# The gate of a top-1 MoE on column groups of TensorE, and GpSimd's two-input work on VectorE

## The chip, the cores and the metric

One core of a Trainium2 chip runs the whole kernel. The metric is the device time of one execution in microseconds; lower is better. TensorE is called PE here, VectorE DVE, ScalarE ACT, GpSimd POOL and SyncE, which issues most DMAs, SP, as in the profile.

## The reference

Three layers follow one another, for B = 4 batches, H = 8 heads, S = 768 positions, D = 48, so 3072 tokens of 384 numbers:

```python
state = f[:, :, t, :, None] * state + einsum('bhd,bhe->bhde', k[:, :, t], v[:, :, t])  # f = sigmoid(f_logit)
y[:, :, t] = einsum('bhd,bhde->bhe', q[:, :, t], state)
...
h = x @ w_in                        # 384 -> 2048
x = (h * sigmoid(h)) @ w_out        # 2048 -> 384
...
logits = x @ w_gate                 # 384 -> 8 experts
expert_idx = argmax(logits, axis=1)
gate_w = softmax(logits)[arange(N), expert_idx]
for e in range(8):                  # each token goes to one expert only
    out[mask] = gate_w[mask, None] * (np.maximum(x[mask] @ w1[e], 0.0) @ w2[e])   # 384 -> 1024 -> 384
```

All inputs and outputs are fp32.

## The kernel before

The tokens are cut into 24 chunks of 128 (n = 0 to 23), and the chunks into nine groups g of 2, 2, 3, 3, 3, 3, 3, 3 and 2 chunks, which are called tiles t of their group. The middle layer of a group takes 16 slots, one for each 128 columns of `w_in`. In a slot (`moe_h`, `moe_g`, `moe_o`) PE computes nine `ph` records, ACT and DVE turn them into the activated values `sg` and split these into a high part `gh` (a cast on ACT, L513) and a low part `gl` (a subtraction on DVE, L514), and PE multiplies them into `px` two slots later. Every weight and value is split that way (`w_hi`, `w_lo`; `xth`, `xtl`), and three products stand for one.

The attention layer, the loads and the routing are functions that a table (`at`, `at_end`, from L1093) puts into slots. PE's instructions keep the order in which the program issues them; for DVE, ACT, POOL and SP a scheduler chooses an order beforehand, and each then works in order. `ph` has two PSUM banks, `px` three, and all else three.

When a group's `px` is complete, `moe_x2` copies its tiles to SBUF. Then, one tile a slot, `flip_rows` turns a tile with three PE transposes into a PSUM bank `plt` and ACT copies it to `rt` (L579); `gate`, at the end of the same slot, multiplies the turned tile by the gate's weights `wgc` (L582 to L586):

```python
for c in range(KC):
    pe.matmul(pt[:, DM : DM + E], rt[:, c, :], wgc[:, c, :], start=c == 0, stop=c == KC - 1)
nc.vector.tensor_copy(lgt[g][:, t, :], pt[:, DM : DM + E])
```

The first operand of a matmul behind the output is the stationary one, the second the moving one. So `rt`, 128 by 128, is stationary, and 8 columns move; an fp32 matmul is two records in the trace. One slot behind the last tile `pick` finds each token's expert with small DVE operations (and an Exp on ACT), and RD = 4 slots later `route` counts the ranks on PE and scatters each token's row into `xs` in DRAM (a POOL DMA, L666). The last group, 8, takes other functions (`logits_pe`, `logits_pe2`).

`load_expert_unit` loads pieces of an expert's weights (`w_raw`, by SP), casts them on ACT (L228) and subtracts (L229). In slots 4, 6, 8 and 10 of group 8 it does so for expert 0, and `preload` behind the slots for half of expert 1; both give POOL the subtraction. `head_fetch`, in slot HF0 = 137 (slot 9 of group 8), reads the first rows of the first expert, `xe_h`, from `xs` (SP), and DVE casts their token numbers, `oi_h` (L775). `head_turn` turns these rows on PE (`pxs_h`).

POOL also multiplies the attention's state by the decay (L465, for n in `STP`, 1 to 7; 10 instructions) and makes `xtl` from n = 7 on (L477, 17 instructions).

Of the kernel before, what the change touches and what calls it, by code (L numbers as in the profile page):

```python
# [9 lines left out]
F32 = mybir.dt.float32  # L10
# [22 lines left out]
FC = 3  # L33
ORD = 1
AMP = ()
STP = (1, 2, 3, 4, 5, 6, 7)
PI = 12
PO = 12
LF = -27
# [47 lines left out]
FAR = float(1 << 20)  # L87
HEAD = 2
YT = 7
YLO = 1  # L90
CAPS = 512, 480, 432, 416, 400, 384, 376, 368
TINY = 2.0**-15

# [2 lines left out]
def kernel(  # L96
# [46 lines left out]
    def bank(kind, name):  # L143
        return ps.tile([P, 512], F32, tag=kind, name=name, bufs={"h": 2, "x": 3, "a": 3}[kind])
# [15 lines left out]
    state_all = state[:, : NPR * 112].rearrange("p (r e) -> p r e", r=NPR)  # L160
    qpads = [const.tile([P, H, 64], F32, name=f"qpad{i}") for i in range(2)]
    kpads = [const.tile([P, H, 64], F32, name=f"kpad{i}") for i in range(2)]
    wgc = const.tile([P, KC, E], F32, name="wgc")
    big = late.tile([P, 6 * 512], F32R, tag="big", name="big")
    xt0 = [big[:, i * 2 * DM : (i + 1) * 2 * DM].rearrange("p (r c t) -> p r c t", r=2, c=KC) for i in range(2)]
    zrow = big[:, 4 * DM : 4 * DM + ROW].bitcast(F32)
# [242 lines left out]
    def att4(n):  # L409
# [47 lines left out]
        for j in range(2):  # L457
            rows, cols = slice(64 * j, 64 * j + D), slice(0, D)
            ab = a_all[rows, n, :, None].to_broadcast([D, NPR, D])
            s = state_all[rows, :, 64 * j : 64 * j + D]  # L460
            if first:
                nc.vector.tensor_tensor(out=s, in0=pu3[rows, :, cols], in1=ab, op=ALU.mult)
            else:
                nc.vector.tensor_tensor(out=s, in0=pu3[rows, :, cols], in1=s, op=ALU.add)
                (nc.gpsimd if n in STP else nc.vector).tensor_tensor(out=s, in0=s, in1=ab, op=ALU.mult)  # L465

    def att5(n):
        g, r = group_of[n]
        if r == 0:
            xt[g] = xt0 if g == 0 else tuple(  # L470
                att.tile([P, CPG, KC, P], F32R, tag=f"xt{s}", name=f"xt{s}_{g}", bufs=2) for s in ("h", "l")
            )
        xh, xl = xt[g]
        y = ysb.pop(n)
        if n >= YT:
            nc.scalar.copy(xh[:, r], y)
            (nc.gpsimd if YLO else nc.vector).tensor_sub(xl[:, r], y, xh[:, r].bitcast(F32))  # L477
            return
        pt = use(n, 7, f"pt_{n}")
        for c in range(KC):  # L480
            pe.transpose(pt[:, c * P : (c + 1) * P], y[:, c, :], ident)
        pt3 = pt[:, :DM].rearrange("p (c t) -> p c t", c=KC)
        nc.scalar.copy(xh[:, r], pt3)
        nc.vector.tensor_sub(xl[:, r], pt3, xh[:, r].bitcast(F32))  # L484
# [76 lines left out]
    def logits_pe2(g):  # L561
        for t, rt in enumerate(rts):
            pl = bank(LB, f"plg_{g}_{t}")
            for c in range(KC):
                pe.matmul(pl[:, :E], rt[:, c, :], wgc[:, c, :], start=c == 0, stop=c == KC - 1)
            nc.vector.tensor_copy(lgt[g][:, t, :], pl[:, :E])

    flipped = {}
# [2 lines left out]
    def flip_rows(g, t):  # L571
        r = x2[starts[g] + t]
        pt = bank("a", f"plt_{g}_{t}")
        for c in range(KC):
            pe.transpose(pt[:, c * P : (c + 1) * P], r[:, c * P : (c + 1) * P], ident)
        if not turned_rows:
            turned_rows.append(late.tile([P, 4, KC, P], F32, tag="big", name="rt"))
        rt = turned_rows[0][:, (starts[g] + t) % 4]
        nc.scalar.copy(rt.rearrange("p c t -> p (c t)"), pt[:, :DM])  # L579
        flipped[g, t] = pt, rt  # L580

    def gate(g, t):  # L582
        pt, rt = flipped.pop((g, t))
        for c in range(KC):
            pe.matmul(pt[:, DM : DM + E], rt[:, c, :], wgc[:, c, :], start=c == 0, stop=c == KC - 1)
        nc.vector.tensor_copy(lgt[g][:, t, :], pt[:, DM : DM + E])  # L586

    picked = {}

# [336 lines left out]
    def general():  # L926
# [44 lines left out]
        with tc.tile_pool(name="g2", bufs=1) as gp, tc.tile_pool(name="g2p", bufs=1, space=PSUM) as pp:  # L971
# [17 lines left out]
            with tc.For_i(0, NT, P) as n0:  # L989
# [29 lines left out]
                x2T = flip(xr, "x2T")  # L1019
                pl = pp.tile([P, 512], F32, name="pl")  # L1020
                for c in range(KC):
                    nc.tensor.matmul(pl[:, :E], x2T[:, c, :], wgc[:, c, :], start=c == 0, stop=c == KC - 1)
                sh = gp.tile([P, E], F32, name="sh")
                oh = gp.tile([P, E], F32, name="oh")
                mx = gp.tile([P, 1], F32, name="mx")
# [41 lines left out]
    def consts():  # L1067
# [58 lines left out]
    for g in range(NG - 1):  # L1126
        s0 = {0: L0, 1: L1}.get(g, pos[g, NF - 1] + LAG + 1)
        for t in range(sizes[g]):
            at(s0 + t, flip_rows, g, t)
            at_end(s0 + t, gate, g, t)  # L1130
        s0 += sizes[g]
        at(s0, pick, g)
        at(s0 + RD, route, g)
        if g == NG - 3:
            at(s0 + RD + 1, rank_first)
            at(s0 + RD + 3, lambda: load_ids(ranks[0], (0, 1)))
# [5 lines left out]
    at(HF0, head_fetch)  # L1142
    at(NG * NF - 1, head_turn)
    for j in range(4):
        at(NG * NF - NF + 4 + 2 * j, load_expert_unit, (("w1", "w2")[j // 2], 0, j % 2), nc.gpsimd)
    at(6, lambda: nc.sync.dma_start(out=wgc, in_=moe2_w_gate.rearrange("(c p) e -> p c e", p=P)))

    def empty_row():
        tc.keep_in_program_order(nc.gpsimd.memset(zrow, 0.0))
# [52 lines left out]

    def preload():
        for j in range(2):
            load_expert_unit(("w1", 1, j), nc.gpsimd)

    todo = dict(
        o=lambda: moe_o(*outs.pop(0)), f=lambda: fill(1), F=lambda: fill(len(ops)), l=lambda: logits_pe(g),
# [52 lines left out]
```

## Time and profile before

| | |
|---|---|
| median of 3 runs | 857.5 us (854.74 to 859.63) |
| profiled execution, its own time | 856.19 us |
| its span | 854.5 us |
| mean granted clock of PE | 0.984 |
| busy: PE, DVE, ACT, POOL | 96%, 56%, 44%, 13% |

The span is the time from the first to the last instruction of the profiled execution; some 1.7 us of its own time lie around it. The shares are means over stages with different limits, so the table by stretches and the waits of PE say more of where time can go or come from.

### The profile page before, as it was taken

Reading aid. Unit: us, or ns where it says so; the run is one execution under the profiler, and the core shown is the slowest. Engines: PE = TensorE matmul, PEld = TensorE weight load, DVE = VectorE, ACT = ScalarE, POOL = GpSimd, SP = SyncE. Lnnn points to the kernel's source line nnn. Section 1 sums busy time; section 2 is a strip of 40 time slices with the busy share of each in tenths; the row PEclk is TensorE's granted clock in tenths of the full one; section 3 lists DMA queues with packets and bytes.
Section 4 is the critical chain, followed back from the end, with each engine's and each line's share of the span. In section 5 each row is a group of like instructions: output and inputs, shape, how many; then the busy total and the mean of one; then the engine's idle time right before and its main releaser. Section 6 shows DMA issues by size and latency. Waiting matters only on the chain.

```text
span 854.5 us, 15384 instructions
## 1 busy us (share of the span) xinstructions
PE 820.2 (96%) x5684; PEld 780.3 (91%) x5684; DVE 477.0 (56%) x1256; ACT 376.3 (44%) x797; POOL 109.2 (13%) x144
## 2 busy tenths in 40 slices
PE   7789999989999999999999999998999999999994
PEld 4679899989999999999999999998999999999994
DVE  4989965555565556566566556354465426336520
ACT  3565464353353453435435333355264435435520
POOL 2010000001001001001001001055301110110001
PEclk9899899999999999999999999999999999999997
DMA  9866773312334244344334322214182515525400
GB/s 185 184 154 167 225 218 96 65 33 80 91 79 124 61 85 121 75 84 113 83 77 109 86 56 83 67 38 159 51 292 70 183 53 195 177 78 181 158 25 27
DMA packets 166435, 95.92 MB, mean 112 GB/s; under 512 B 115692, under 2 KB 159965, under 8 KB 166352
## 3 DMA queue, kind: packets, MB, share of 16 engines
q1 hardware_dynamic: 162224, 83.80, 37.8%
q0 software_dynamic: 3280, 9.49, 3.1%
q10 hardware_dynamic: 848, 1.57, 0.6%
q8 instruction: 46, 0.75, 0.4%
q14 instruction: 37, 0.30, 0.1%
HBM read 75.61 MB, written 16.33 MB: 108 GB/s over the span
## 4 chain that ended last, share of the span: by engine, by line
PE 71%; DMA 9%; DVE 6%; issue 6%; ACT 5%; SPq 2%; POOL 1%; POOLq 0%; DVEq 0%; ACTq 0%
PE ph L335 19%; PE px L335 19%; PE po L335 8%; PE p L335 7%; PE py L335 5%; DMA out_dram<-o,oi 3%; DMA f<-in_f_logit_dram 3%; PE sc L335 2%; DMA w_raw<-in_moe_w_dram 2%; PE pl L335 1%; PE plt L335 1%; PE pk L340 1%; PE pq L340 1%; PE p_r L335 1%; PE po_r L335 1%
## 5 line engine op out<-in xcount | busy, mean ns | idle before, releaser
L503 ACT ACTIVATE se<-ph 128x384 f32<-128x384 f32 (+1 forms) x144 | 65.5, 455 | 177.6 <-PE ph L335 171.0
L505 DVE SCALAR_TENSOR_TENSOR sg<-se,ph 128x384 f32<-128x384 f32 (+1 forms) x144 | 73.1, 508 | 115.4 <-ACT se L503 112.6
L335 PE MATMUL px<-out_lo,gh 128*128 128x384 f32 x384 | 137.3, 358 | 0.0
L335 PE MATMUL px<-out_hi,gl 128*128 128x384 f32 x384 | 129.8, 338 | 0.4 <-DVE gl L514 0.4
L335 PE MATMUL px<-out_hi,gh 128*128 128x384 f32 x384 | 129.6, 337 | 0.0
L335 PE MATMUL ph<-xtl,in_hi 128*128 128x384 f32 (+1 forms) x384 | 126.1, 328 | 1.6 <-DVE xtl L484 1.6
L335 PE MATMUL ph<-xth,in_hi 128*128 128x384 f32 (+1 forms) x384 | 124.8, 325 | 0.0
L335 PE MATMUL ph<-xth,in_lo 128*128 128x384 f32 (+1 forms) x384 | 124.4, 324 | 0.0
L514 DVE TENSOR_TENSOR gl<-sg,gh 128x384 fp32r<-128x384 f32 (+1 forms) x144 | 82.4, 572 | 36.9 <-ACT gh L513 35.9
L513 ACT CAST gh<-sg 128x384 fp32r<-128x384 f32 (+1 forms) x144 | 68.6, 477 | 67.4 <-DVE sg L505 62.6
L335 PEld LDWEIGHTS px<-out_lo,gh 128*128 128x128 f32 x384 | 72.4, 189 | 2.6 <-issue 0.2
L335 PEld LDWEIGHTS ph<-xtl,in_hi 128*128 128x128 f32 x384 | 72.9, 190 | 2.0 <-DVE xtl L484 1.9
L335 PEld LDWEIGHTS px<-out_hi,gl 128*128 128x128 f32 x384 | 72.6, 189 | 1.0 <-DVE gl L514 0.6
L335 PEld LDWEIGHTS ph<-xth,in_lo 128*128 128x128 f32 x384 | 72.9, 190 | 0.0
L335 PEld LDWEIGHTS ph<-xth,in_hi 128*128 128x128 f32 x384 | 72.8, 190 | 0.0
L335 PEld LDWEIGHTS px<-out_hi,gh 128*128 128x128 f32 x384 | 72.3, 188 | 0.0
L335 PE MATMUL po<-w_lo,hh 128*128 128x384 f32 (+6 forms) x200 | 67.8, 339 | 0.0
L335 PE MATMUL po<-w_hi,hh 128*128 128x384 f32 (+6 forms) x200 | 67.2, 336 | 0.0
L335 PE MATMUL po<-w_hi,hl 128*128 128x384 f32 (+6 forms) x200 | 67.2, 336 | 0.0
L228 ACT CAST w_hi<-w_raw 128x384 fp32r<-128x384 f32 x124 | 57.2, 513 | 21.8 <-DMA w_raw<-in_moe_w_dram 19.5
L229 DVE TENSOR_TENSOR w_lo<-w_raw,w_hi 128x384 fp32r<-128x384 f32 x104 | 52.6, 552 | 10.6 <-ACT w_hi L228 10.4
L335 PE MATMUL p<-xsl,w_hi 128*128 128x480 f32 (+6 forms) x168 | 58.5, 348 | 0.0
(240 smaller groups left out, 1506.3 us busy)
## 6 DMA issues: line engine op xcount, KB each, us to landing
w_raw<-in_moe_w_dram SPq DMA_DIRECT2D x64, 384.0 KB
xs<-big SPq DMA_DIRECT2D x8, 776.0 KB
out_again<-in_moe_w_out_dram SPq DMA_DIRECT2D x16, 384.0 KB
xe<-xs SPq DMA_DIRECT2D x7, 776.0 KB
out_raw<-in_moe_w_out_dram SPq DMA_DIRECT2D x13, 384.0 KB
f<-in_f_logit_dram SPq DMA_DIRECT2D x24, 192.0 KB
k<-in_k_dram SPq DMA_DIRECT2D x24, 192.0 KB
q<-in_q_dram SPq DMA_DIRECT2D x24, 192.0 KB
```

Of the source, the lines that this page charges most:

```text
L228: (keep(nc.scalar.copy) if key == ("w1", 1, 1) and RT > 1 else nc.scalar.copy)(hi[:, h], x)
L229: lo_engine.tensor_sub(lo[:, h], x, hi[:, h].bitcast(F32))
L335: ins = nc.tensor.matmul(*a, **k)
L340: ins = nc.tensor.transpose(*a, **k)
L503: nc.scalar.activation(e, ph[:, :GT], AF.Tanh, scale=0.5)
L505: nc.vector.scalar_tensor_tensor(out=t, in0=e, scalar=1.0, in1=ph[:, :GT], op0=ALU.add, op1=ALU.mult)
L513: (nc.scalar.copy if g < GACT else nc.vector.tensor_copy)(hi, t)
L514: (nc.gpsimd if (g, i) < LOV else nc.vector).tensor_sub(lo, t, hi.bitcast(F32))
```

## The change

The gate's weights become the stationary operand. `wgc` is now 128 x 3 x 32, zero behind its 8 columns. At the end of the slot of a group's last flip, `gate(g)` multiplies them with all tiles of the group as moving operand, tile t writing partitions 32t to 32t + 31 of one bank `pg`; ACT copies these 96 (or 64) partitions to `lt`, which has its place in the `rt` buffer. At the end of the next slot `gate_rows` turns them with one PE transpose, and DVE copies the logits. `pick`, `route` and what hangs on them stand one slot later than before. The state product, `xtl` and the expert weights' `w_lo` go from POOL to DVE. Lines move by a few: L335 and L340 (PE) are L333 and L338, L579 is L577.

```diff
@@ -33,7 +33,6 @@
 FC = 3
 ORD = 1
 AMP = ()
-STP = (1, 2, 3, 4, 5, 6, 7)
 PI = 12
 PO = 12
 LF = -27
@@ -87,7 +86,6 @@
 FAR = float(1 << 20)
 HEAD = 2
 YT = 7
-YLO = 1
 CAPS = 512, 480, 432, 416, 400, 384, 376, 368
 TINY = 2.0**-15
 
@@ -160,7 +158,7 @@
     state_all = state[:, : NPR * 112].rearrange("p (r e) -> p r e", r=NPR)
     qpads = [const.tile([P, H, 64], F32, name=f"qpad{i}") for i in range(2)]
     kpads = [const.tile([P, H, 64], F32, name=f"kpad{i}") for i in range(2)]
-    wgc = const.tile([P, KC, E], F32, name="wgc")
+    wgc = const.tile([P, KC, 32], F32, name="wgc")
     big = late.tile([P, 6 * 512], F32R, tag="big", name="big")
     xt0 = [big[:, i * 2 * DM : (i + 1) * 2 * DM].rearrange("p (r c t) -> p r c t", r=2, c=KC) for i in range(2)]
     zrow = big[:, 4 * DM : 4 * DM + ROW].bitcast(F32)
@@ -462,7 +460,7 @@
                 nc.vector.tensor_tensor(out=s, in0=pu3[rows, :, cols], in1=ab, op=ALU.mult)
             else:
                 nc.vector.tensor_tensor(out=s, in0=pu3[rows, :, cols], in1=s, op=ALU.add)
-                (nc.gpsimd if n in STP else nc.vector).tensor_tensor(out=s, in0=s, in1=ab, op=ALU.mult)
+                nc.vector.tensor_tensor(out=s, in0=s, in1=ab, op=ALU.mult)
 
     def att5(n):
         g, r = group_of[n]
@@ -474,7 +472,7 @@
         y = ysb.pop(n)
         if n >= YT:
             nc.scalar.copy(xh[:, r], y)
-            (nc.gpsimd if YLO else nc.vector).tensor_sub(xl[:, r], y, xh[:, r].bitcast(F32))
+            nc.vector.tensor_sub(xl[:, r], y, xh[:, r].bitcast(F32))
             return
         pt = use(n, 7, f"pt_{n}")
         for c in range(KC):
@@ -577,13 +575,27 @@
             turned_rows.append(late.tile([P, 4, KC, P], F32, tag="big", name="rt"))
         rt = turned_rows[0][:, (starts[g] + t) % 4]
         nc.scalar.copy(rt.rearrange("p c t -> p (c t)"), pt[:, :DM])
-        flipped[g, t] = pt, rt
-
-    def gate(g, t):
-        pt, rt = flipped.pop((g, t))
+        flipped[g, t] = rt
+
+    gated = {}
+
+    def gate(g):
+        m = 32 * sizes[g]
+        pg = bank("a", f"pg_{g}")
         for c in range(KC):
-            pe.matmul(pt[:, DM : DM + E], rt[:, c, :], wgc[:, c, :], start=c == 0, stop=c == KC - 1)
-        nc.vector.tensor_copy(lgt[g][:, t, :], pt[:, DM : DM + E])
+            for t in range(sizes[g]):
+                pe.matmul(
+                    pg[32 * t : 32 * t + 32, :P], wgc[:, c, :], flipped[g, t][:, c, :], start=c == 0, stop=c == KC - 1
+                )
+        lt = turned_rows[0][:, (starts[g] + 3) % 4, 0, :]
+        nc.scalar.copy(lt[:m], pg[:m, :P])
+        gated[g] = pg, lt
+
+    def gate_rows(g):
+        pg, lt = gated.pop(g)
+        m = 32 * sizes[g]
+        pe.transpose(pg[:, P : P + m], lt[:m], ident[:m, :m])
+        nc.vector.tensor_copy(lgt[g], pg[:, P : P + m].rearrange("p (t e) -> p t e", e=32)[:, :, :E])
 
     picked = {}
 
@@ -1077,6 +1089,7 @@
         for t in qpads + kpads:
             nc.gpsimd.memset(t, 0.0)
         nc.gpsimd.memset(state, 0.0)
+        nc.gpsimd.memset(wgc, 0.0)
         nc.gpsimd.memset(a_all, 1.0)
         nc.gpsimd.memset(base, 0.0)
         nc.gpsimd.memset(wmin, 1.0)
@@ -1127,8 +1140,10 @@
         s0 = {0: L0, 1: L1}.get(g, pos[g, NF - 1] + LAG + 1)
         for t in range(sizes[g]):
             at(s0 + t, flip_rows, g, t)
-            at_end(s0 + t, gate, g, t)
         s0 += sizes[g]
+        at_end(s0 - 1, gate, g)
+        at_end(s0, gate_rows, g)
+        s0 += 1
         at(s0, pick, g)
         at(s0 + RD, route, g)
         if g == NG - 3:
@@ -1142,8 +1157,8 @@
     at(HF0, head_fetch)
     at(NG * NF - 1, head_turn)
     for j in range(4):
-        at(NG * NF - NF + 4 + 2 * j, load_expert_unit, (("w1", "w2")[j // 2], 0, j % 2), nc.gpsimd)
-    at(6, lambda: nc.sync.dma_start(out=wgc, in_=moe2_w_gate.rearrange("(c p) e -> p c e", p=P)))
+        at(NG * NF - NF + 4 + 2 * j, load_expert_unit, (("w1", "w2")[j // 2], 0, j % 2), nc.vector)
+    at(6, lambda: nc.sync.dma_start(out=wgc[:, :, :E], in_=moe2_w_gate.rearrange("(c p) e -> p c e", p=P)))
 
     def empty_row():
         tc.keep_in_program_order(nc.gpsimd.memset(zrow, 0.0))
@@ -1202,7 +1217,7 @@
 
     def preload():
         for j in range(2):
-            load_expert_unit(("w1", 1, j), nc.gpsimd)
+            load_expert_unit(("w1", 1, j), nc.vector)
 
     todo = dict(
         o=lambda: moe_o(*outs.pop(0)), f=lambda: fill(1), F=lambda: fill(len(ops)), l=lambda: logits_pe(g),
```

What is left out takes the first 8 columns of the wider `wgc` in two other functions.

The first place is PE at the end of the slot of the last flip of group 7, slot 4 of group 8 (`plt_7_2` is the third tile's turned bank, `ph_8_5` the next slot's first product). Before:

```order
L340 MATMUL plt_7_2_6779<-ident_77,x2_21_6695 128x128 x3
L335 MATMUL px_8_0_6720<-out_0_lo_213,gh_8_2_6716 128x384
L335 MATMUL px_8_0_6720<-out_0_hi_212,gl_8_2_6717 128x384
L335 MATMUL px_8_0_6720<-out_0_hi_212,gh_8_2_6716 128x384
L335 MATMUL px_8_1_6721<-out_0_lo_213,gh_8_2_6716 128x384
L335 MATMUL px_8_1_6721<-out_0_hi_212,gl_8_2_6717 128x384
L335 MATMUL px_8_1_6721<-out_0_hi_212,gh_8_2_6716 128x384
L335 MATMUL plt_7_2_6779<-wgc_90,rt_2039 128x8 x3
L335 MATMUL ph_8_5_6812<-xtl_8_6199,in_1_hi_415 128x256
L335 MATMUL ph_8_5_6812<-xth_8_6198,in_1_lo_416 128x256
```

The change, at the same place:

```order
L338 MATMUL plt_7_2_6781<-ident_77,x2_21_6705 128x128 x3
L333 MATMUL px_8_0_6730<-out_0_lo_214,gh_8_2_6726 128x384
L333 MATMUL px_8_0_6730<-out_0_hi_213,gl_8_2_6727 128x384
L333 MATMUL px_8_0_6730<-out_0_hi_213,gh_8_2_6726 128x384
L333 MATMUL px_8_1_6731<-out_0_lo_214,gh_8_2_6726 128x384
L333 MATMUL px_8_1_6731<-out_0_hi_213,gl_8_2_6727 128x384
L333 MATMUL px_8_1_6731<-out_0_hi_213,gh_8_2_6726 128x384
L333 MATMUL pg_7_6810<-rt_2040,wgc_90 32x128 x9
L333 MATMUL ph_8_5_6821<-xtl_8_6207,in_1_hi_416 128x256
```

and at the end of the next slot:

```order
L333 MATMUL px_8_1_6731<-out_0_lo_214,gh_8_3_6757 128x384
L333 MATMUL px_8_1_6731<-out_0_hi_213,gl_8_3_6758 128x384
L333 MATMUL px_8_1_6731<-out_0_hi_213,gh_8_3_6757 128x384
L338 MATMUL pg_7_6810<-ident_77,rt_2040 128x96
L333 MATMUL ph_8_6_6847<-xtl_8_6207,in_1_hi_416 128x256
L333 MATMUL ph_8_6_6847<-xth_8_6206,in_1_lo_417 128x256
```

One stationary `rt` per tile with 8 moving columns has become one block of nine matmuls (18 records) for three tiles, and a transpose stands a slot behind it.

The second place is ACT in slots 5 to 7 of group 8 (`w1_0_1` and `w2_0_0` are units of expert 0). Before:

```order
L503 ACTIVATE se_8_5_6822<-ph_8_5_6812 128x256
L228 CAST w1_0_1_hi_6865<-w1_0_1_raw0_6867 128x384 x2
L228 CAST w1_0_1_hi_6865<-w1_0_1_raw1_6873 128x384 x2
L513 CAST gh_8_5_6841<-sg_8_5_6824 128x256
L503 ACTIVATE se_8_6_6861<-ph_8_6_6851 128x256
L513 CAST gh_8_6_6879<-sg_8_6_6863 128x256
L228 CAST w2_0_0_hi_6927<-w2_0_0_raw0_6929 128x384 x2
L503 ACTIVATE se_8_7_6899<-ph_8_7_6889 128x256
L228 CAST w2_0_0_hi_6927<-w2_0_0_raw1_6935 128x384 x2
L513 CAST gh_8_7_6903<-sg_8_7_6901 128x256
L503 ACTIVATE se_8_8_6923<-ph_8_8_6913 128x256
L513 CAST gh_8_8_6941<-sg_8_8_6925 128x256
```

The change:

```order
L501 ACTIVATE se_8_5_6831<-ph_8_5_6821 128x256
L226 CAST w1_0_1_hi_6876<-w1_0_1_raw0_6878 128x384 x2
L226 CAST w1_0_1_hi_6876<-w1_0_1_raw1_6884 128x384 x2
L511 CAST gh_8_5_6835<-sg_8_5_6833 128x256
L501 ACTIVATE se_8_6_6857<-ph_8_6_6847 128x256
L623 ACTIVATE r_sh_7_6863<-r_sh_7_6863 128x24
L226 CAST w2_0_0_hi_6938<-w2_0_0_raw0_6940 128x384 x2
L501 ACTIVATE se_8_7_6910<-ph_8_7_6900 128x256
L226 CAST w2_0_0_hi_6938<-w2_0_0_raw1_6946 128x384 x2
L511 CAST gh_8_6_6890<-sg_8_6_6859 128x256
L501 ACTIVATE se_8_8_6934<-ph_8_8_6924 128x256
L511 CAST gh_8_7_6914<-sg_8_7_6912 128x256
```

`gh_8_6` stands behind the four casts of `w2_0_0` and `se_8_7`, where it stood ahead of them; `r_sh_7` of `pick` is a slot later.

The third place is DVE in the same slots (`oi_h` waits for the fetch `xe_h`, L227 is `w_lo`). Before:

```order
L646 TENSOR_TENSOR r_off_7_6840<-r_off_7_6840,r_lim_7_6965 128x3
L647 TENSOR_SCALAR r_lim_7_6965<-r_lim_7_6965 128x3
L514 TENSOR_TENSOR gl_8_5_6842<-sg_8_5_6824,gh_8_5_6841 128x256
L505 SCALAR_TENSOR_TENSOR sg_8_6_6863<-se_8_6_6861,ph_8_6_6851 128x256
L514 TENSOR_TENSOR gl_8_6_6880<-sg_8_6_6863,gh_8_6_6879 128x256
L505 SCALAR_TENSOR_TENSOR sg_8_7_6901<-se_8_7_6899,ph_8_7_6889 128x256
```

The change:

```order
L503 SCALAR_TENSOR_TENSOR sg_8_4_6779<-se_8_4_6777,ph_8_4_6767 128x256
L512 TENSOR_TENSOR gl_8_4_6801<-sg_8_4_6779,gh_8_4_6800 128x256
L503 SCALAR_TENSOR_TENSOR sg_8_5_6833<-se_8_5_6831,ph_8_5_6821 128x256
L787 CAST oi_h_0_7467<-xe_h_6976 128x1
L787 CAST oi_h_1_7514<-xe_h_6976 128x1
L598 COPY lg_7_6700<-pg_7_6810 128x24
L227 TENSOR_TENSOR w1_0_1_lo_6877<-w1_0_1_raw0_6878,w1_0_1_hi_6876 128x384
L612 TENSOR_REDUCE r_mx_7_6861<-lg_7_6700 128x3
L227 TENSOR_TENSOR w1_0_1_lo_6877<-w1_0_1_raw0_6878,w1_0_1_hi_6876 128x384
L614 TENSOR_TENSOR r_sh_7_6863<-lg_7_6700,r_mx_7_6861 128x24
L227 TENSOR_TENSOR w1_0_1_lo_6877<-w1_0_1_raw1_6884,w1_0_1_hi_6876 128x384 x2
L616 SCALAR_TENSOR_TENSOR r_oh_7_6865<-r_sh_7_6863,e_rev3_97 128x24
```

Between `sg_8_5` and `gl_8_5` stand now the two casts of `oi_h`, the first pieces of `pick` and four `w_lo`, where two small pieces of `route` stood.

## Rows read from the trace of the kernel before

**Rows 1.** Page, part 1: busy us, share of the span and instructions of each engine.

```profile
PE 820.2 (96%) x5684; PEld 780.3 (91%) x5684; DVE 477.0 (56%) x1256; ACT 376.3 (44%) x797; POOL 109.2 (13%) x144
```

**Rows 2.** Table by stretches: us, busy PE, PEld, DVE, ACT, POOL, then clock, DMA share, GB/s.

```profile
60.00:100.00 40.00, 36.79 (x289) 35.29 (x287) 38.88 (x94) 20.38 (x49) 2.94 (x7) 0.97 0.69 189
...
240.00:400.00 160.00, 159.56 (x1182) 153.56 (x1181) 95.36 (x263) 73.30 (x138) 15.89 (x15) 1.00 0.39 90
...
560.00:580.00 20.00, 19.01 (x144) 18.64 (x143) 12.41 (x41) 11.14 (x31) 14.76 (x14) 1.00 0.17 51
580.00:600.00 20.00, 17.77 (x122) 16.19 (x121) 8.49 (x24) 11.17 (x29) 12.29 (x13) 1.00 0.50 160
```

**Rows 3.** Timeline of PE, waits: start, us, work [idle before <-releaser].

```profile
95.96 0.43 PE L335 MATMUL py<-state,qt 112*128 112x96 f32 x2 [1.55 <-DVE am L406]
...
178.27 0.84 PE L335 MATMUL plt<-wgc,rt 128*128 128x8 f32 x6 [2.56 <-ACT rt L579]
...
561.70 0.83 PE L335 MATMUL plt<-wgc,rt 128*128 128x8 f32 x6 [0.99 <-ACT rt L579]
...
589.80 0.44 PE L340 MATMUL pxs_h<-ident,xe_h 128*128 128x128 f32 x2 [1.18 <-DVE sg L505]
```

**Rows 4.** Table by stretches behind two of these waits (columns as in rows 2).

```profile
97.00:105.00 8.00, 8.00 (x37) 7.65 (x36) 7.83 (x19) 3.06 (x8) 0.31 (x1) 0.57 0.78 225
179.00:183.00 4.00, 4.00 (x18) 3.98 (x18) 0.72 (x2) 0.50 (x2) 0.00 (x0) 0.57 0.02 4
```

**Rows 5.** Timeline of PE around one tile's gate.

```profile
557.47 0.73 PE L335 MATMUL plt<-wgc,rt 128*128 128x8 f32 x6
558.05 0.36 PE L335 MATMUL ph<-xtl,in_hi 128*128 128x256 f32 x1
558.26 0.28 PE L335 MATMUL ph<-xth,in_lo 128*128 128x256 f32 x1
558.37 0.28 PE L335 MATMUL ph<-xth,in_hi 128*128 128x256 f32 x1
```

**Rows 6.** Timeline of PE in one `att4`: full array, then column halves, then full.

```profile
533.55 1.04 PE L335 MATMUL py<-qt,state 112*112 112x128 f32 x8
534.51 1.08 PE L335 MATMUL py<-am,v 128*48 128x128 f32 x16
535.52 0.45 PE L335 MATMUL px<-out_lo,gh 128*128 128x384 f32 x1
535.81 0.33 PE L335 MATMUL px<-out_hi,gl 128*128 128x384 f32 x1
535.98 0.34 PE L335 MATMUL px<-out_hi,gh 128*128 128x384 f32 x1
```

**Rows 7.** Timeline of ACT before the wait at 178.27.

```profile
174.92 1.28 ACT L503 ACT_TABLE_LOAD   x1
```

**Rows 8.** Groups by line, engine and shape (busy us, mean ns); last, one DVE timeline row.

```profile
L229 POOL TENSOR_TENSOR w_lo<-w_raw,w_hi 128x384 fp32r<-128x384 f32 x24 | 25.0, 1079 | 27.4 <-ACT w_hi L228 19.9 <-PE pxs_h L340 7.5
...
L229 DVE TENSOR_TENSOR w_lo<-w_raw,w_hi 128x384 fp32r<-128x384 f32 x104 | 52.6, 552 | 10.6 <-ACT w_hi L228 10.4
...
L465 DVE TENSOR_TENSOR state<-state,a_all 48x192 f32<-48x192 f32 x22 | 7.7, 351 | 0.4
...
61.01 0.86 DVE L229 TENSOR_TENSOR in_lo<-in_cv,in_hi 128x384 fp32r<-128x384 f32 x1
```

**Rows 9.** Timeline, the end of the first phase: SP's queue, DVE, ACT, PE.

```profile
582.96 0.37 SPq L201 DMA_DIRECT2D xe_h<-xs  x1
...
586.04 0.21 DVE L775 CAST oi_h<-xe_h 128x1 int32<-128x1 f32 x2 [2.36 <-DMA xe_h<-xs]
...
567.55 1.76 ACT L228 CAST w_hi<-w_raw 128x384 fp32r<-128x384 f32 x4 [0.26 <-PE px L335]
...
570.23 0.41 DVE L514 TENSOR_TENSOR gl<-sg,gh 128x256 fp32r<-128x256 f32 x1
...
570.86 0.34 PE L335 MATMUL px<-out_lo,gh 128*128 128x384 f32 x1
```

More of the change, by code (lines that the diff above doesn't have):

```diff
@@ L564, in logits_pe2 @@
             for c in range(KC):
-                pe.matmul(pl[:, :E], rt[:, c, :], wgc[:, c, :], start=c == 0, stop=c == KC - 1)
+                pe.matmul(pl[:, :E], rt[:, c, :], wgc[:, c, :E], start=c == 0, stop=c == KC - 1)
             nc.vector.tensor_copy(lgt[g][:, t, :], pl[:, :E])
@@ L1021, in general @@
                 for c in range(KC):
-                    nc.tensor.matmul(pl[:, :E], x2T[:, c, :], wgc[:, c, :], start=c == 0, stop=c == KC - 1)
+                    nc.tensor.matmul(pl[:, :E], x2T[:, c, :], wgc[:, c, :E], start=c == 0, stop=c == KC - 1)
                 sh = gp.tile([P, E], F32, name="sh")
```

## The prediction

> **What bounds the kernel now.** I read the busy shares first. TensorE is busy 96% of the span [rows 1], so a gain has to be PE work that goes or PE idle time that goes. The stretches then say where idle time is left [rows 2]: 240 to 400 us is full (159.56 of 160), with DVE at 95.36, that is 60%; 60 to 100 has 36.79 of 40, with DVE at 38.88, so there DVE is the limit; 560 to 580 lacks 1 us and 580 to 600 lacks 2.2. The PE timeline gives the waits one by one [rows 3]. Two of them, 2.56 us at 178.27 and 0.99 at 561.70, stand before a gate record `plt<-wgc,rt`, which the change removes. A long wait can also cost what comes after it: from 179 to 183 us the granted clock is 0.57, so mostly the lower of the two levels (1.2 of 2.4 GHz), and so it is from 97 to 105, after the wait at 95.96 [rows 4].
>
> **The gate's matmuls, today.** Each of 22 tiles issues six records: a 128x128 weight load, then 8 moving columns. From the first record to the next `ph` is 558.05 - 557.47 = 0.58 us, or 0.097 a record, and that `ph` is followed 0.21 later where 0.11 is the rule, 0.10 more [rows 5]. That is 0.68 a tile, rounded down to 0.67 for what a `ph` would have shown anyway; 22 x 0.67 = 14.7 us, all of it on PE in full stretches.
>
> Here the Trainium skill, "TensorEngine Tiling (Array Packing)", section Instruction Overhead, says that a matmul costs some 60 cycles however few columns it has. As an estimate from that page, 60 cycles at 2.4 GHz are 0.025 us, the old gate would be 132 x 0.025 + 22 x 0.10 = 5.5 us, and the change would lose about 4.6. No run here shows such a price; 0.097 for the same record is measured, so the measurement decides.
>
> **The gate's matmuls, after.** 132 records again: 18 in each of six groups of three tiles, 12 in each of two groups of two. Each has 32 weight columns and 128 moving columns, and the tiles take turns on the column groups. No such record is in the trace. The nearest: full-array records of 128 columns, `py<-qt,state`, come every (534.51 - 533.55)/8 = 0.12 us; records on alternating column halves, `py<-am,v`, every (535.52 - 534.51)/16 = 0.063, so two halves run beside each other; and leaving that mode costs 0.29 where 0.17 is the rule, 0.12 more [rows 6]. Upper bound: no overlap, 0.12. Lower bound: three tiles share one such time, 0.042. I take 0.05 for three tiles (between 0.042 and the 0.063 of two) and 0.063 for two. A group also pays about 0.2 for going in and out and about 0.2 for the transpose back (a 0.12 record and its re-entry). Three tiles: 18 x 0.05 + 0.4 = 1.3; two: 12 x 0.063 + 0.4 = 1.16; together 6 x 1.3 + 2 x 1.16 = 10.1. **Term: -4.6 us** (bounds +4.3 with 132 x 0.12 + 3.2 = 19.0, and -5.5).
>
> The ACT copy and the DVE copy per group (8 of each) replace 22 DVE copies. ACT is busy 44% [rows 1], and the transpose back stands a slot behind the gate, so I cost the copies at nothing; without that slot between them PE would wait out a copy in each of eight groups.
>
> **The wait at 178.27.** The gate of group 0's first tile stands at the end of the flip's own slot, while ACT loads a table (1.28 us, beginning at 174.92) and comes to the copy `rt` only after that [rows 7, 3]. After the change nothing on PE reads that `rt` until one slot later, about 4 us, and the second copy has its 9 `px` records (1.6 us) as cover. What is late next is the `gh` of that slot, wanted two slots on. **Term: -2.56 and 4.00 x (1 - 0.57) = 1.7 of clock, -4.3 us.**
>
> **The wait at 561.70.** The same on group 7's second tile, behind weight casts on ACT; the gate now follows the third flip. **Term: -1.0 us.**
>
> **GpSimd's work on DVE: the middle.** 17 `xtl` and 24 `w_lo` at 0.55, 10 state products at 0.35 [rows 8]: 26 us. From 240 to 400 us DVE is 60% busy and PE is full, so I cost the `xtl` there at nothing; `xth` on ACT, for which `xtl` now holds DVE's queue, already holds ACT's own. Without that cover each would cost up to 0.55, 9.4 us in all.
>
> **The start.** Two pairs of state products (n = 3 and 4) fall into the stretch where DVE is full. On DVE a pair costs 2 x 0.351 = 0.70. On GpSimd it slows DVE beside it: `in_lo` took 0.86 where 0.552 is usual [rows 8], with smaller stretches near it some 0.4 in all. Net +0.3 a pair, two pairs. **Term: +0.6 us** (from -3 to +4: a wait like that at 95.96 cost 1.55 and 8.00 x 0.43 = 3.4 of clock, and one could come or go).
>
> **The end of the first phase.** Three things move. `route` of group 7 now stands behind `head_fetch`, so `xe_h` on SP waits only for the scatters of group 6; today SP sits until 582.96, DVE stands 2.36 before `oi_h` [rows 9], and PE later waits 1.18 at 589.80 [rows 3] and shorter in other places, 2.2 in all from 580 to 600 [rows 2]. About 2.1 of it goes. In exchange twelve `w_lo` of expert 0's first units stand in DVE's row between `sg` and `gl`. Call T the end of `px` in slot 5 of group 8. Four `w_hi` take 1.76 from about T [rows 9]. On DVE four `w_lo` and three small pieces end at T + 3.1, and `gl` of slot 5 at T + 3.5. In the trace it began at 570.23 for the `px` at 570.86, T + 3.2 [rows 9]: a wait of some 0.2. The `w2_0_0` casts need the weights that `ph` of slot 7 frees (T + 3.2); with a `se` between they end at T + 5.4, their `w_lo` at about T + 6, and `gl` of slot 6 at T + 6.5, wanted at T + 5.4: a wait of 1.1. So -2.1 + 1.3. **Term: -0.8 us** (from -2.1 to +5, if each of the four units costs such a wait or a fetch in SP's row comes late).
>
> **Sum:** -4.6 - 4.3 - 1.0 - 0.8 + 0.6 = -10.1. The profiled execution took 856.19 us, so 846.1; the median of the runs, 857.5, stands 1.3 above it. Forecast **847.4 us**.
>
> **Rivals.**
> 1. *Column groups of this kind don't overlap.* Three tiles read three different moving streams, which no row shows. For it: only halves are seen, with 48 columns. Against: the halves do overlap. Gate +4.3 in place of -4.6: 847.4 + 8.9 = **856.3**, no change.
> 2. *DVE becomes the limit at the start or in group 8.* A slot of group 8 has nine `ph` records of 0.11 and six `px` of 0.17, some 2.1 us, and DVE's queue is in order. If the end costs +4 and the start +2, then 847.4 + 4.8 + 1.4 = **853.6**. For it: the 38.88 of 40, and the waits that I worked out above. Against: GpSimd's own slowness (1.08 a `w_lo`) goes, and with it small DVE operations slowed by it.
> 3. *Slower: PE drains at each change of column group.* Each record then takes its 0.12 and the 0.12 of a change of mode: 132 x 0.24 + 3.2 = 35 us against 14.7, so 847.4 + 4.6 + 20.3 = **872.3**. It decides as soon as a record takes over 0.16 us (132 x 0.16 + 3.2 is 9.7 over today, which eats the rest of the gain, 5.5, and 0.5% more). Against it: 0.063 at alternating halves. For it: a change of tile with the output in a third or fourth group isn't in the trace.
> 4. *The wait at 178 only moves.* ACT's row is the same Exp, Ln and two table loads, with one more small copy. If PE meets it one slot on: 847.4 + 4.3 = **851.7**.
>
> **How the numbers follow.** Half a per cent, 4.3 us, is about what a measurement of this kernel can tell from no change: faster is below 853.2, slower above 861.8. Forecast 0.60, rival 1 0.10, rival 2 0.14, rival 3 0.04, rival 4 0.12. Faster: 0.60 + 0.12 + half of rival 2 = 0.79. Slower: rival 3 and 0.01 of rival 2 (an end at +5 with clock lost behind its waits) = 0.05. Same: 0.16. Range: below, the gate at -5.5, the end at -2.1 and the start at -3 give 847.4 - 0.9 - 1.3 - 3.6 = 841.6; above, it takes in rivals 4 and 2 and stops short of most of rival 1: 841 to 855.5. It leaves out rivals 1 and 3 and a little of the rest, under 0.2.
>
> **What would show it.** Right: `pg<-rt,wgc` records some 0.05 us apart; no wait of PE near 178 and a clock of 1.00 behind it; `xe_h` issued near 565; PE idle about 1.3 between 560 and 600. Wrong: records 0.12 apart or more (rivals 1, 3); new waits of PE on DVE's `gl`, `xtl` or `am` (rival 2); clock below 1 in stretches where it is 1.00 today.

## The result, and the profile after

The changed kernel takes 847.23 us (median of 4 runs, 845.27 to 847.92); the kernel before took 856.66 beside it (4 runs). The ratio is 0.990, with a 95% interval of 0.9878 to 0.9921: about 1% faster, where 847.4 us was forecast. The profiled execution took 845.27 us, the fastest of the four, with a span of 843.6.

The page of the changed kernel, part 1 (busy us, share of the span, instructions), against [rows 1]:

```profile
PE 810.5 (96%) x5692; PEld 766.8 (91%) x5692; DVE 483.4 (57%) x1293; ACT 377.1 (45%) x805; POOL 59.1 (7%) x94
```

PE has 9.7 us less to do and is as full as before. DVE is busy only 6.4 us more, although it took over work that was priced at 26 us there: beside a POOL that does less, its own `gl` of 384 columns take 0.555 us on average, where they took 0.632, 7.4 us in all.

The table by stretches of the changed kernel (columns as in [rows 2]); 178 to 183 answers to [rows 4]:

```profile
178.00:183.00 5.00, 5.00 (x36) 4.55 (x36) 2.73 (x8) 1.70 (x5) 0.00 (x0) 1.00 0.34 81
560.00:580.00 20.00, 18.33 (x131) 17.42 (x131) 16.71 (x57) 12.30 (x33) 3.24 (x3) 1.00 0.46 149
580.00:600.00 20.00, 19.55 (x146) 18.64 (x145) 11.34 (x58) 6.06 (x18) 1.94 (x2) 1.00 0.11 35
```

At 178 there is no wait and the clock is 1.00. Between 560 and 600 us PE is idle 2.1 (3.2 before; the prediction had about 1.3), of which the timeline of PE shows the two new waits that the prediction had placed there, next to one in the middle that it had not:

```profile
538.28 0.45 PE L333 MATMUL ph<-xtl,in_hi 128*128 128x384 f32 x1 [0.87 <-DVE sg L503]
...
561.31 0.44 PE L333 MATMUL px<-out_hi,gl 128*128 128x384 f32 x1 [0.45 <-DVE gl L512]
...
565.11 0.45 PE L333 MATMUL px<-out_hi,gl 128*128 128x384 f32 x1 [1.22 <-DVE gl L512]
```

The new gate in the timeline of PE, first a group of two tiles, then one of three, each with the `px` ahead and the `ph` behind:

```profile
163.70 0.34 PE L333 MATMUL px<-out_hi,gh 128*128 128x384 f32 x1
163.97 0.87 PE L333 MATMUL pg<-rt,wgc 128*32 128x128 f32 x12
164.77 0.44 PE L333 MATMUL ph<-xtl,in_hi 128*128 128x384 f32 x1
...
554.23 0.85 PE L333 MATMUL pg<-rt,wgc 128*32 128x128 f32 x18
555.01 0.39 PE L333 MATMUL ph<-xtl,in_hi 128*128 128x256 f32 x1
```

18 records take 555.01 - 554.23 = 0.78 us, 0.043 each; 12 records take 0.80. Three tiles cost what two cost: the lower bound of the prediction, three column groups side by side.

**One table for all runs.** In the timeline of PE I took two marks in each profiled execution, the first `ph` of group 2 and that of group 8, and so have three stretches: the start, the middle (groups 2 to 7), and the end (all behind). In us:

```
kernel                          start   middle   end    span   median of runs
before                          142.1   407.7   304.7   854.5   855.6 to 856.7 (in each comparison)
the change                      139.6   401.9   302.1   843.6   847.23
e1_gate_only                    142.1   401.5   310.5   854.1   855.68
e2_dve_only                     142.8   409.1   304.9   856.8   859.59
e3_state_pool                   142.2   401.7   302.2   846.1   847.25
e4_xtl_pool                     142.4   402.0   302.8   847.2   849.30
e5_wlo_pool                     142.2   402.1   310.6   854.9   856.13
e10_gate_wlo                    141.2   401.4   303.0   845.6   847.29
e7_rd3                          139.9   401.6   300.9   842.5   845.44
e6_one_group                    139.9   409.7   302.3   851.9   855.76
e9_tile_by_tile                 142.4   404.7   302.4   849.5   849.95
e8_gate_together                140.5   407.7   303.2   851.4   855.50
e11_no_second_read              142.3   398.0   302.9   843.1   845.21
e12_before_no_second_read       141.4   407.2   306.0   854.6   856.19
```

For the change the sum reads -2.5 at the start, -5.8 in the middle and -2.6 at the end, against +0.6, -8.2 (all gates but the last, and the wait at 178) and -2.5 (the last gate, the wait at 561.7 and the end's own term) in the prediction. The total fits; two of the three parts do not, with opposite signs. The experiments go after these two, and after which part of the change earns what.

### The profile page after: what moved, and what is told of

Its sections match the earlier page's. It is cut to its first block, busy times and chain, and to the rows that moved or that the text cites. A ratio compares the mean times of both kernels' runs of the same rounds, so it can differ in the third digit from the quotient of the medians.

```text
span 843.6 us, 15324 instructions
## 1 busy us (share of the span) xinstructions
PE 810.5 (96%) x5692; PEld 766.8 (91%) x5692; DVE 483.4 (57%) x1293; ACT 377.1 (45%) x805; POOL 59.1 (7%) x94
## 4 chain that ended last, share of the span: by engine, by line
PE 60%; DMA 12%; issue 10%; DVE 9%; ACT 4%; SPq 3%; POOLq 0%; POOL 0%; DVEq 0%; ACTq 0%
PE px L333 19%; PE ph L333 18%; DMA out_dram<-o,oi 6%; PE py L333 4%; PE po L333 4%; PE p L333 4%; PE sc L333 2%; DMA w_raw<-in_moe_w_dram 1%; DMA f<-in_f_logit_dram 1%; DVE am L404 1%; PE pl L333 1%; PE p_r L333 1%; PE po_r L333 1%; PE pq L338 1%; PE pk L338 1%
## 5 line engine op out<-in xcount | busy, mean ns | idle before, releaser
L333 PE MATMUL px<-out_lo,gh 128*128 128x384 f32 x384 | 137.3, 357 | 0.3 <-ACT gh L511 0.3
L333 PE MATMUL px<-out_hi,gl 128*128 128x384 f32 x384 | 130.2, 339 | 2.2 <-DVE gl L512 2.2
L333 PE MATMUL px<-out_hi,gh 128*128 128x384 f32 x384 | 129.7, 338 | 0.0
L333 PE MATMUL ph<-xtl,in_hi 128*128 128x384 f32 (+1 forms) x384 | 125.5, 327 | 1.2 <-DVE sg L503 0.9
L333 PE MATMUL ph<-xth,in_hi 128*128 128x384 f32 (+1 forms) x384 | 124.0, 323 | 0.0
L333 PE MATMUL ph<-xth,in_lo 128*128 128x384 f32 (+1 forms) x384 | 123.8, 322 | 0.0
L512 DVE TENSOR_TENSOR gl<-sg,gh 128x384 fp32r<-128x384 f32 (+1 forms) x144 | 73.4, 510 | 29.2 <-ACT gh L511 28.1
L333 PEld LDWEIGHTS ph<-xtl,in_hi 128*128 128x128 f32 x384 | 72.5, 189 | 3.8 <-issue 1.4
L333 PEld LDWEIGHTS px<-out_hi,gl 128*128 128x128 f32 x384 | 72.6, 189 | 3.6 <-DVE gl L512 3.2
L333 PEld LDWEIGHTS px<-out_lo,gh 128*128 128x128 f32 x384 | 72.4, 188 | 3.2 <-ACT gh L511 0.9
L333 PEld LDWEIGHTS ph<-xth,in_lo 128*128 128x128 f32 x384 | 72.5, 189 | 0.0
L333 PEld LDWEIGHTS ph<-xth,in_hi 128*128 128x128 f32 x384 | 72.4, 189 | 0.0
L333 PEld LDWEIGHTS px<-out_hi,gh 128*128 128x128 f32 x384 | 72.3, 188 | 0.0
L227 DVE TENSOR_TENSOR w_lo<-w_raw,w_hi 128x384 fp32r<-128x384 f32 x128 | 65.1, 552 | 12.5 <-ACT w_hi L226 11.8
L333 PE MATMUL po<-w_lo,hh 128*128 128x384 f32 (+6 forms) x200 | 67.8, 339 | 0.0
L333 PE MATMUL po<-w_hi,hh 128*128 128x384 f32 (+6 forms) x200 | 67.2, 336 | 0.0
L333 PE MATMUL po<-w_hi,hl 128*128 128x384 f32 (+6 forms) x200 | 67.2, 336 | 0.0
L333 PE MATMUL p<-xsl,w_hi 128*128 128x480 f32 (+6 forms) x168 | 58.5, 348 | 0.0
```

Source lines behind the costliest of these rows:

```text
L227: lo_engine.tensor_sub(lo[:, h], x, hi[:, h].bitcast(F32))
L333: ins = nc.tensor.matmul(*a, **k)
L512: (nc.gpsimd if (g, i) < LOV else nc.vector).tensor_sub(lo, t, hi.bitcast(F32))
```

## The experiments

**The new gate alone.** STATE, XTL and W_LO name three edits that give work back to POOL; here all three:

```diff
-                nc.vector.tensor_tensor(out=s, in0=s, in1=ab, op=ALU.mult)
+                (nc.gpsimd if 1 <= n <= 7 else nc.vector).tensor_tensor(out=s, in0=s, in1=ab, op=ALU.mult)   # STATE
-            nc.vector.tensor_sub(xl[:, r], y, xh[:, r].bitcast(F32))
+            nc.gpsimd.tensor_sub(xl[:, r], y, xh[:, r].bitcast(F32))   # XTL
-... load_expert_unit, (("w1", "w2")[j // 2], 0, j % 2), nc.vector)   (and in preload)
+... load_expert_unit, (("w1", "w2")[j // 2], 0, j % 2), nc.gpsimd)   # W_LO
```

> The change's gate, with the state products, xtl and w_lo left on POOL. Read from the two traces so far, slot by slot: the gate's matmuls and transposes save about 5.5 us, the two waits on rt with the clock behind one of them 5.2, the start 2.5, and the middle groups give back about 3. Theory A: the loss in the middle comes from xtl on DVE, the gain at the start from the state products on DVE. Then this kernel has neither: 856.7 - 10.7 = 846.0, and group 2's first ph stands at 142, as before. Theory B: the loss in the middle comes with the gate, since pick, route and the expert loads stand a slot later: 856.7 - 10.7 + 3 = 849.0, with the same start. My prediction's own terms (gate -4.6, waits -5.3, nothing else): 846.8.

855.68 us, ratio 0.9988 (0.997 to 1.0007): no gain. All of it is lost at the end, +5.8 against before and +8.4 against the change. The timeline of its DVE, POOL and PE shows one place:

```profile
576.88 0.97 POOL L678 DMA_INDIRECT xs<-x,r_idx  x1 [0.30 <-issue]
577.88 7.67 POOL L227 TENSOR_TENSOR w_lo<-w_raw,w_hi 128x384 fp32r<-128x384 f32 x8
...
577.31 8.52 DVE L512 TENSOR_TENSOR gl<-sg,gh 128x256 fp32r<-128x256 f32 x1 [0.47 <-ACT gh L511]
...
585.89 0.69 PE L333 MATMUL px<-out_hi,gl 128*128 128x384 f32 x1 [6.47 <-DVE gl L512]
```

A DVE subtraction that takes 0.43 lasted 8.52 us: it began beside a POOL scatter and ended 0.28 behind the last of eight `w_lo` that followed without a gap. PE waited 6.47, and the granted clock behind that is at and near the lower of its two levels (1.2 of 2.4 GHz):

```profile
584.00:588.00 4.00, 2.11 (x7) 0.50 0.00 0
588.00:592.00 4.00, 4.00 (x23) 0.68 0.01 2
```

(Columns: stretch, busy PE, clock, DMA share, GB/s.) None of the three expectations had this; the middle, 401.5, is Theory B's (the loss in the middle comes with the gate, not with `xtl`).

**The work on DVE alone**, with the old gate (`STP = ()`, `YLO = 0`, both `nc.gpsimd` of the `w_lo` to `nc.vector`):

> The gate as before, but all two-input work of POOL on DVE. Theory A (xtl on DVE costs 2 to 3 in the middle, the state products gain 2.5 at the start): 856 to 857, group 2's first ph at 139.6. Theory B (only the start gains): 854.2. My prediction's terms (start +0.6, end -0.8, middle 0): 856.5, with group 2's first ph at 142.7. In all three the wait of PE at about 178 stays.

859.59 us, ratio 1.0032 (1.0011 to 1.0053): slightly slower. The start is 142.8, so the move does not shorten it; the middle is 1.4 longer. Each half of the change by itself brings nothing, and together they bring 9 us.

**One part of POOL's work at a time.** The change with STATE:

> The change, with the ten state products back on POOL. If they made the start 2.5 us shorter, 847.2 + 2.5 = 849.7 and group 2's first ph at 142.1. If the start's gain has another cause (the order of the start's work came out another way, the memset of wgc), 847.2 and 139.6. My prediction had the products cost 0.6 on DVE: 846.6.

847.25: no difference from the change. Its start is 142.2, but its median is not 2.5 higher. The change with XTL:

> The change, with the 17 xtl back on POOL. Theory A: the 2 to 3 us that the middle groups lost come back, 844.5 to 845. Theory B: 847.2, with the waits of PE on DVE's am and on sg (0.87 us at 538) still there.

849.30 (ratio 0.9868 to 0.994, which overlaps the change's): the 3 us do not come back, and the middle is the same 402.0. Theory A falls. The change with W_LO:

> The change, with only the 24 w_lo of expert 0 and of half of expert 1 back on POOL. In the run with the new gate alone, one DVE gl (two SBUF inputs) lasted 8.52 us while POOL ran eight w_lo without a gap, PE waited 6.47 for it, and the clock was at its lower level behind that. Theory L: back-to-back w_lo on POOL hold up that DVE operation; then this kernel is at 855 to 857 with the same long gl near 577, though state products and xtl are on DVE. Rival: the loss came from the state products or xtl on POOL, or was chance of that kernel's order: 847.2, no DVE gl over 1.5 us.

856.13, ratio 1.0002 (0.9991 to 1.0014): the whole gain is gone, and the same row stands there, in DVE's and POOL's timeline:

```profile
577.95 8.51 DVE L512 TENSOR_TENSOR gl<-sg,gh 128x256 fp32r<-128x256 f32 x1 [0.47 <-issue]
...
578.50 7.67 POOL L227 TENSOR_TENSOR w_lo<-w_raw,w_hi 128x384 fp32r<-128x384 f32 x8
```

Theory L holds in the time and in the long `gl`, but back-to-back `w_lo` alone do not make one: the kernel before has eight of them without a gap, and `gl` came through in between. What the long ones share is a scatter. In the 14 profiles a `gl` lasts over 1.4 us eleven times, and each began beside a POOL scatter that a POOL subtraction followed at once; nine met a single `xtl` and lasted 2.03 to 2.05, and these two met eight `w_lo`. One more `gl` in that place lasted only 0.56 (e8_gate_together, 464.86). POOL and DVE of the kernel before, first the row of `w_lo`, then a scatter and an `xtl`:

```profile
568.30 8.88 POOL L229 TENSOR_TENSOR w_lo<-w_raw,w_hi 128x384 fp32r<-128x384 f32 x8 [4.39 <-ACT w_hi L228]
...
571.45 0.43 DVE L514 TENSOR_TENSOR gl<-sg,gh 128x256 fp32r<-128x256 f32 x1 [0.47 <-ACT gh L513]
...
262.72 0.97 POOL L666 DMA_INDIRECT xs<-x,r_idx  x1 [0.30 <-issue]
263.72 1.02 POOL L477 TENSOR_TENSOR xtl<-y,xth 128x384 fp32r<-128x384 f32 x1
...
263.13 2.03 DVE L514 TENSOR_TENSOR gl<-sg,gh 128x384 fp32r<-128x384 f32 x1
```

In the two kernels with the new gate and `w_lo` on POOL, the scatters of group 7 stand right ahead of eight `w_lo`; in the kernel before, the next `w_lo` begins 7.5 us behind them. No run changes this order by itself, so the scatter's part is read from the rows only.

The change with STATE and XTL, so that only the `w_lo` are on DVE:

> The new gate, and of POOL's work only the w_lo on DVE; state products and xtl stay on POOL. Theory L: the w_lo are the one part of that move that matters: 846 to 848, as the whole change. If xtl and state products on DVE matter as well: their parts show in the ledger of slots, over 849.

847.29, ratio 0.9894: as the whole change. The `w_lo` are the one part of the move that matters; the state products and `xtl` could have stayed.

**Route back in its old slot.**

```diff
-RD = 4
+RD = 3
-HF0 = 137
+HF0 = 136
```

> The change, with RD = 3 and HF0 = 136, so that route, rank_first and the expert's loads stand in their old slots (only pick is a slot later), and the fetch of xe_h still waits only for group 6. From group 2's first ph to group 8's the change gained 5.7 us, where its gate and the wait at 178 gained 8.8 by the single slots; with xtl on POOL it was the same. Theory B: the 3 us are lost because route and what hangs on it moved by a slot: 844 to 845 and a gain of some 8 between the two marks. Rival: they are lost by the order on DVE in general (reductions that wait for a DMA ahead of am): 847, gain 5 to 6.

845.44, ratio 0.9874 (0.9858 to 0.9891). The middle is 401.6, a gain of 6.1 where Theory B had some 8, so the slot of `route` is not what cost the 3 us, except at one place: the wait of 0.87 at 538 is gone, and the two slots around it are 1.1 us shorter. In the change ACT's `xth` waits there for data whose DMAs SP issued right behind loads of expert weights, which the later `rank_first` had put off (SP issues them from 526.25 on, and from 521.76 in this run):

```profile
536.65 0.51 ACT L474 CAST xth<-y 128x384 fp32r<-128x384 f32 x1 [5.38 <-DMA y<-yt]
```

The end is 1.2 shorter. This is the lowest median of a version that computes everything; its interval overlaps the change's, so the 1.8 us between the medians are likely, not settled.

**Column groups.** All tiles on one group:

```diff
-        for c in range(KC):
-            for t in range(sizes[g]):
+        for t in range(sizes[g]):
+            for c in range(KC):
...
-                    pg[32 * t : 32 * t + 32, :P], ...
+                    pg[:32, t * P : t * P + P], ...
...
-        pe.transpose(pg[:, P : P + m], lt[:m], ident[:m, :m])
+        for t in range(sizes[g]):
+            pe.transpose(pg[:, DM + 32 * t : DM + 32 * t + 32], lt[:32, t * P : t * P + P], ident[:32, :32])
```

> The change, but every tile on the same column group (partitions 0 to 31 of the bank, one tile after the other along its columns), with a transpose for each tile. In the change 18 records took 0.78 us and 12 took 0.80, so 0.13 for a pair of records whatever the number of tiles. If that is overlap between column groups, here each record takes 0.12 to 0.13: 2.3 us a group of three, 1.5 more than in the change, 0.8 more for two; with the additional transposes 847.2 + 10.7 + 2 = 860. If the records are quick for another reason (32 weight columns only), 848 to 849 with records some 0.045 apart.

855.76, 8.5 over the change. And the groups kept, but with the loops exchanged as above (`for t`, then `for c`):

> The change with the two gate loops exchanged: all three c of one tile, then the next tile, so a column group gets six records in a row before the next group's begin. If only records that alternate between groups overlap, 18 records take 2.1 us, as on a single group (2.08 there): 847.2 + 8 = 855. If each group has a queue of its own, the time stays 0.8 a group of three: 847.2.

849.95. The block of 18 in the timelines of PE, first on one group, then on three, tile by tile:

```profile
562.29 2.15 PE L333 MATMUL pg<-rt,wgc 128*32 128x128 f32 x18
564.37 0.38 PE L333 MATMUL ph<-xtl,in_hi 128*128 128x256 f32 x1
```

```profile
559.78 1.34 PE L333 MATMUL pg<-rt,wgc 128*32 128x128 f32 x18
561.05 0.38 PE L333 MATMUL ph<-xtl,in_hi 128*128 128x256 f32 x1
```

2.08, 1.27 and (in the change) 0.78 us for the same 18 records: 0.116, 0.071, 0.043. On one group the new records are no quicker than the old ones (0.097). The overlap between column groups is the saving, and the order in which records alternate decides how much of it is had. Both expectations were too coarse: the additional transposes cost less than the 2 us that I put in, and the exchanged loops fall between the two cases.

**Only the waits on rt.** The kernel before, with

```diff
-            at_end(s0 + t, gate, g, t)
+            at_end(s0 + min(t + 1, sizes[g] - 1), gate, g, t)
```

> The kernel before with its old gate, but each tile's gate one slot later, at the latest with the group's last, and pick where it was: of the change only the two waits on rt go. By my prediction's terms 2.56 + 1.7 of clock at 178 and 1.0 at 561.7: 856.3 - 5.3 = 851.0, with no PE wait near 178 and the clock at 1.00 there. Rival (the wait only moves): 855 to 856, with a wait on rt or gh one slot on.

855.50, ratio 0.9992 (0.9968 to 1.0015). The wait at 178 is gone, the clock there is 1.00, and that slot is 3.4 us shorter (a slot is taken from its first `ph` to that of the next). But the flipped tile's bank `plt` is now held a slot longer, and six groups pay for that, each with a wait like this in PE's timeline:

```profile
226.72 0.44 PE L335 MATMUL pl<-lfh,trir 128*128 128x384 f32 x1 [0.33 <-ACT yt L436]
```

With that and late `am`, the middle is 407.7 again. So the rival (the wait only moves) is wrong about 178 and right about the sum. The changed gate avoids it: it needs no PSUM between flip and gate.

**The second read of the weights.** `verify_piece` reads the middle layer's weights once more, and DVE reduces them; in the next two runs both are left out (a `return` at its head). The change without it, and the kernel before without it:

> The change without verify_piece: the second read of the middle layer's weights and the DVE reductions that wait for it are left out. Theory V: the 3 us that the middle does not gain are PE waits on am, which DVE makes late because such a reduction stands ahead of it in DVE's row and waits for its DMA; in the kernel before the same waits stand in other slots and are smaller. Then from group 2's first ph to group 8's this kernel gains 8 to 9 us over its own kernel before (the next run), where the change gained 5.7. Rival: the loss has nothing to do with these reductions; the gain stays 5.5 to 6.5.

> The kernel before, with the same second read and its reductions left out: what the run above is compared with. Theory V: the slots with an am late are then all near 5.56 us in both kernels, and this one is 1 to 3 us faster than the kernel before between the marks, the run above 4 to 6 faster than the change. Rival: both win the same.

845.21 and 856.19. The middle is 398.0 against 407.2: a gain of 9.2, where the full kernels gain 5.8. No PE wait over 0.2 us is left between 250 and 540 in either; the kernel before has none there with the reads, and the change has 0.27 and 0.87. With the reads, the change has a row like this in DVE's timeline, with `am` behind it and PE waiting for `am`:

```profile
379.57 0.55 DVE L260 TENSOR_REDUCE wmin<-out_again 128x1 f32<-128x384 f32 x1 [1.19 <-DMA out_again<-in_moe_w_out_dram]
380.04 1.28 DVE L404 TENSOR_TENSOR am<-sc,trir 128x512 f32<-128x512 f32 x2
```

```profile
380.78 0.42 PE L333 MATMUL py<-am,v 128*48 128x128 f32 x2 [0.27 <-DVE am L404]
381.38 1.07 PE L333 MATMUL py<-am,v 128*48 128x128 f32 x14 [0.18 <-DVE am L404]
```

Theory V holds in what it says of the gain. Of its side claims two fail: the kernel before wins only 0.5 in the middle without the reads, not 1 to 3, and in neither kernel are the slots with a late `am` all near 5.56 us (up to 6.3 in both). The change wins 3.9 in the middle, just short of 4. What the two runs leave out is the reads and the reductions together, so they do not tell which of the two it is; that the reductions do it is read from rows like the four above.

## Why the prediction was right

The forecast was right in time and direction. By its terms:

- **Gate, -4.6.** Under-sized. The records of a group of three now cost 0.78 and not 0.90; slot by slot such a group gains 0.91 us (group 3's tiles, in the slots of group 4: 0.57 and 0.68 for two old gates that go, then -0.22 for the block in place of the third and -0.12 for the transpose), one of two tiles about nothing. Six groups give some -5.4, near the lower bound. Records without overlap (rival 1), tried in e6_one_group, would have taken the gain away: 855.76 against the 856.3 of that rival. Rival 3, a drain at each change of group, is excluded by the 0.78.
- **The wait at 178, -4.3.** Right: the two slots in question are 4.7 shorter, of which some 0.3 is the gate, and the clock is at 1.00. With the old gate moved by a slot (e8_gate_together) the same wait and the same lost clock go. Rival 4 did not come.
- **The wait at 561.7, -1.0.** Right: that slot gains 1.9, of which 0.7 is the old gate that goes.
- **The end, -0.8.** About right: the stretch behind group 8's first `ph` is 2.6 shorter, and without the gate and the wait above some 0.5 of that is left. `xe_h` is issued at 553.88 on SP (582.96 before, forecast near 565), and the waits from 580 to 600 fall from 2.2 to 0.45, where 2.1 was to go. The two new waits on `gl`, forecast as 0.2 and 1.1 in slots 7 and 8 of group 8, came as 0.45 and 1.22. What the text did not see is what the term would have been without it. I had priced the move of the `w_lo` against the kernel before, in which no `gl` lasted over 2.05 us; against the new gate with `w_lo` on POOL it is worth 8.9 us (856.13 to 847.23). That the new gate needed this was not foreseen, so the term came out right by luck. A part of a change has to be priced beside the other parts, in the order of work that they make together.
- **The start, +0.6.** Not seen: with the state products on POOL (e3_state_pool) and on DVE (e5_wlo_pool) the start is 142.2. The profiled execution of the change is 2.5 us shorter there, but the change is not the reason: up to the mark e5_wlo_pool has the same instructions in the same order as the change on PE, DVE, ACT and POOL, and still takes 142.2. What differs first is how long PE's early matmuls take. Before and change, second pair of `pl` in the program:

```profile
10.92 1.65 PE L335 MATMUL pl<-f,trir 128*128 128x384 f32 x2 [1.17 <-ACT f L321]
```

```profile
10.66 0.91 PE L333 MATMUL pl<-f,trir 128*128 128x384 f32 x2 [0.77 <-ACT f L319]
```

Of the 14 profiles six show 0.91 there and eight 1.65, with either gate; the six start in 139.6 to 142.1, the eight in 141.4 to 142.8. PE's clock is the likely reason, but shown only in part: from 10.6 to 13 us the granted clock is 0.50, the lower level, in four of the eight and 0.95 in one of the six (e10_gate_wlo); in the nine others, the two above among them, the row reads 1.00 whatever the time. Nor does this alone settle the start: e1_gate_only and e10_gate_wlo show 0.91 and start in 142.1 and 141.2. So the 10.9 us between the two spans hold some 2.5 that are not the change's; the medians differ by 9.4. What sets the early matmuls' speed stays open.
- **The middle, 0 for the work on DVE.** "DVE is 60% busy and PE is full, so I cost the `xtl` there at nothing" came true beside the new gate: 402.0 with `xtl` on POOL (e4_xtl_pool), 401.9 without. Beside the old gate the move made the middle 1.4 longer (e2_dve_only). The step that failed is that nothing else in the middle would answer to the new gate, for which the prediction has no term: gates and wait gained 8.9 there by their slots, and 3.1 of it were given back, 2.0 in the slots with `am` and 1.1 around the wait at 538. Leaving out the second read brings them back, so the second read with its reductions is shown as the cause; that it works through the reductions that wait for their DMA in DVE's row is read from the rows, for `am` alone. Moving `route` back also ends the wait at 538, but then the slots with `am` lose more (e7_rd3). Why the second read hurts the new gate more than the old one is argued only: PE comes sooner to the same `py`, while the DMA lands no sooner. A mean share of 60% says nothing about one operation that stands behind a wait.
- **Rival 2 (DVE becomes the limit), 853.6.** It came in part. Its signs are there, new waits of PE on `gl` and on `am`, but they cost less than its 6.2 us, and the start shows no cost.

Without the start the profiles differ by 8.4 us; the medians differ by 9.4, and 10.1 was forecast. The gate's 0.8 more and a start that cost nothing made up for a part of the middle's 3 less. That the median came out within 0.2 of 847.4 is luck: errors of opposite sign, and a kernel before whose median beside the change was 856.66, not the 857.5 that the forecast set out from.

## What to carry to other kernels

Small-output matmuls gained here by making the small operand stationary and giving each tile its own column group, and most where consecutive records go to different groups: 0.116 us a record on one group, 0.071 on three groups one after the other, 0.043 in turns. The small stationary operand on one group gained nothing (855.76). Before work is left on an engine off the critical path, look for what it can hold up: here GpSimd subtractions behind a scatter stopped a 0.43 us VectorE operation for 8.5 us. Undo each part of a change by itself, since two parts that bring nothing alone brought 1% together.

## What the runs showed of the hardware that I had not expected

- A VectorE operation with two SBUF inputs can wait for a whole row of GpSimd operations: 8.52 and 8.51 us in two kernels, beside a scatter and eight `w_lo` of 0.96 us. In the kernel before, with 1.08 us a `w_lo` [rows 8], such operations came through between two of them. The Trainium skill, "SBUF — State Buffer", section "SBUF: two separate sides", describes an exclusive lock that one of the two engines holds for a whole instruction while the other waits. A `gl` that began beside a single `xtl` at 191 in the kernel before agrees: it lasted 1.06 us and ended 0.42 behind the `xtl`. The 8.5 us are longer than any one instruction there, and no run shows what keeps VectorE waiting from one to the next.
- 12 records on two column groups took 0.80 us, 18 on three 0.78, 18 on one 2.08. The Trainium skill, "TensorE: Matmul & The Clock Gate", section "Measured speedup vs the span model", has 2.38 for three column tiles with 512 columns; here, with 128 columns, it is 2.08 / 0.78 = 2.7.
- The early matmuls of PE took 0.91 or 1.65 us a pair in kernels with the same work there, and the first `ph` of group 2 came at 139.6 or 142.2 with the same instructions in the same order.
